# Projections in pairs on the same loaded weights, and a new static order

## The chip, the cores and the metric

The kernel runs on one core of a Trainium2 chip. The metric is the device time of one execution in microseconds, and the median of several runs is compared. The profile and the trace come from one further execution.

## The reference, cut to what matters

Four layers work on a sequence of 2048 tokens of width 512, with a layer norm before each and a residual sum after it: A, B, A, B, all with the same two sets of weights.

Layer A is attention by segments with a memory. The sequence is cut into 64 segments of 32 tokens, and 8 memory tokens stand ahead of each:

```python
for s in range(n_seg):
    h = jnp.concatenate([mem, xs], axis=1)
    q = jnp.einsum('btd,dhe->bhte', h, Wq)      # k and v likewise
    scores = jnp.einsum('bhqe,bhke->bhqk', q, k) * scale
    p = _softmax(jnp.where(mask[None, None], scores, -1000000000.0), axis=-1)
    o = jnp.einsum('bhqk,bhke->bhqe', p, v)
    o = jnp.einsum('bhte,hed->btd', o, Wo)
    mem = o[:, :M, :].copy()
    outs.append(o[:, M:, :])
```

There are 32 heads of 128. The memory of a segment comes out of the segment before it, so the segments form a chain. The memory rows may be seen by every token, and the 32 own tokens are masked causally.

Layer B is linear attention over the whole sequence: a projection to q, k and v (32 heads of 16), a feature map, one sum of k by v over all tokens, and a division.

## The kernel before, in words

**Tiles.** The 32 rows that a segment's step projects (8 memory tokens and the first 24 of its own) are the stationary operand of the matmul, `blk`, in four chunks of 128 features; the last 8 tokens of four segments are gathered into one "left" block of 32 rows, which is projected once for four segments (`left_block`). TensorE's array is used as four strips of 32 columns: a matmul has a `tile_position=(0, 32 * j)`, and four of them, one for each strip, run side by side on different columns of the weight matrix. Such four are called a group below. `project` (L1309) makes one product of 32 rows by 2048 columns, half of Wq, Wk or Wv: for each of the four chunks a group, each matmul with 512 moving columns, all into one PSUM bank. Every `pe.matmul` becomes two instructions of TensorE, a load of the stationary operand (LDWEIGHTS, row PEld in the profile) and the MATMUL itself. Each of the four strips loads the same 32 columns of `blk`.

**Steps of a segment in layer A.** `k0`, `k1`, `q0`, `q1`: the halves of k and q, each projected, evacuated from PSUM (L1150 on ScalarE or L1151 on VectorE) and turned by 32x32 blocks on VectorE (L1341, in `turned`). `v0`, `v1`: the halves of v, projected and evacuated. `mem0`, `mem1`: scores of both halves (L1417, L1423), exponentials, sums over the memory tokens with a matrix of ones as the stationary operand (`sums`, through `tiled`, L1261), and the weighted values. `out`: the projection with Wo (L1560). `next`: picks the memory rows for the next segment (L1584). `res`: residual rows, over a DMA from partition to partition on the GpSimd queue (L1595, L1166). `x`: the attention of the own tokens, off the memory's chain; its `sums` multiply a block matrix of ones, `bo_sb`, with two moving operands, 256 and 64 wide (L1498, L1494). Layer B's steps for each 128 tokens are `bi`, `bo`, `bm`, `bl`.

**What sets the order.** All is unrolled. Every operation has a key (layer, step, name, number), and two tables give each key a time: `PERIOD` for a repeating pattern of four segments, `OWN` for the steps outside it. `schedule` sorts all operations by these times, and that order is written to the five engines; the times have no other use. A letter behind a time says which engine evacuates, `a` for ScalarE and `v` for VectorE. Each engine runs its own list in order and waits on semaphores where an operand comes from another engine. Eight PSUM banks are given out in the order of the list: a tile takes the bank that came free first.

**At the start** the three matrices Wv, Wk and Wq (4 MB each) are fetched by DMAs that ScalarE issues, and Wo by SyncE after them.

Of the kernel before, what the change touches and what calls it, by code (L numbers as in the profile page):

```python
# [19 lines left out]
    0: (44811, 8548, {  # L20
# [3 lines left out]
        'k0': {  # L24
            0: '27075 27835 28266 28482 28937a 29591',
            1: '37951 38167 38382 38813 39593a 40223',
            2: '49129 49776 49991 50207 50833v 51555',
            3: '60060 60275 60491 60922 61377a 62008',
        },
        'k1': {  # L30
            0: '29460 29891 30106 30322 30777a 31461',
            1: '39244 39891 40106 40537 41172a 42855',
            2: '51284 52146 52362 52577 53033a 53663',
            3: '62430 62861 63077 63292 63748a 64508',
        },
        'q0': {
            0: '26213 26644 26860 28051 28506v 29229',
            1: '38598 39029 39460 39675 40382a 41013',
            2: '49560 50422 50853 51069 51524a 52155',
            3: '61137 61353 61784 62215 62670a 63301',  # L40
        },
        'q1': {
            0: '26429 27346 29244 29675 30131v 31099',
            1: '40322 40753 40968 41184 41653a 43217',
            2: '49345 50638 51715 51931 52386a 53137',
            3: '60706 61568 61999 62646 63152a 64146',
        },
        'v0': {
            0: '30537 31971 32314 32530 32985a',
            1: '41399 41743 41958 42174 42629a',  # L50
            2: '51500 52821 53036 53783 54238a',
            3: '63508 63723 63967 64498 65023a',
        },
        'v1': {
            0: '32849 33177 33392 33608 34063a',
            1: '42556 43050 43265 43896 44624a',
            2: '53567 54404 54675 55002 55754a',
            3: '64182 64852 65661 66044 66796a',
        },
        'ql': {  # L60
            0: '29419a 20723a',
            1: '38961a 39431a',
            2: '45732v 45838v',
            3: '56799a 59805a',
        },
# [5 lines left out]
        },  # L71
# [5 lines left out]
        },  # L77
        'out': {
# [4 lines left out]
        },  # L83
        'next': {
            0: '37244 37304 37674a',
            1: '48363 48423 48793a',
            2: '59078 59353 59723a',
            3: '70225 70341 70711a',
        },
        'res': {  # L90
            0: '37280 37736 38286 27562 28697 29026 30881 31099 31317 31535 31753 32211a 32372a 32683 35339 35889 36439 34789 33689 34239 36989 33139 41375',
            1: '48292 49298 48748',
            2: '60782 61788 61238',
            3: '72597 73054 73604',
        },
        'bi': {
            2: '41830 42777 43111 43458 43703 44222 41831 45054v 45612 45829 46275 46491 46947 48745 50087 69577 69794 78810 79242 80554v 82311 70401 91215 70771 81379 81604 81829 82537 83291 83921 84265 87192',
        },
# [5 lines left out]
        },  # L104
        'prep': {
            2: '14773 22863 25330 32839 45393 46045 46515a 51917v 54935a 49318a 49183a',
        },
        'left0': {
            2: '47795 48483 48698 48914 49453a 57204 47579 48147 53252 55489 57604a 58877',
        },  # L110
        'left1': {
            2: '58431 58862 59413 59844 60566a 64870 55273 56159 58647 59629 60084a 65510',
        },
        'leftv0': {
            2: '67011 68054 70010 70587 71042v 72121 75548',
        },
        'leftv1': {
            2: '59138 65445 66546 67226 68217a 76773 77947',
        },
        'lefts': {  # L120
            2: '77556 79138 79889 80348',
        },
    }),
    1: (47082, 762505, {
        'bo': {
            0: '1100 0 6030 6495 7750 10877 15245 17797 18014 18230 19216',
        },
        'k0': {
            0: '7730 8001 8217 8870 9325v 10048',
            1: '19150 19581 19797 20228 20683a 21314',  # L130
            2: '31406 31621 31892 32323 32779a 33409',
            3: '41870 42517 43594 44025 44481a 45111',
        },
        'k1': {
            0: '8432 11035 11466 11785 12241a 12871',
            1: '21736 21952 22167 22383 22838a 23469',
            2: '31190 32108 32970 33185 33641a 35120',
            3: '43810 45402 45617 45833 46288v 47539',
        },
        'q0': {  # L140
            0: '9085 9301 9516 9732 10187a 11484',
            1: '20012 20443 20659 20874 21330a 21960',
            2: '29897 30328 30544 30759 31215a 31845',
            3: '42301 42732 42948 43379 43834a 44465',
        },
        'q1': {
            0: '7299 7515 10819 11250 11706a 12336',
            1: '19366 21090 21305 21521 21997a 22628',
            2: '30113 30975 32539 33672 34127a 34758',
            3: '42086 43163 44241 44727 45590a 47177',  # L150
        },
        'v0': {
            0: '13105 13348 13664 13879 14335a',
            1: '22598 22842 23268 23484 23939a',
# [877 lines left out]
def _build_kernel(nc, A_x, A_mem0, A_Wq, A_Wk, A_Wv, A_Wo, A_seg_len, B_wqkv, B_wo, out):  # L1032
# [112 lines left out]
    add = P.add  # L1145
# [742 lines left out]
```

## Time and profile before

| what | value |
|---|---|
| median of 3 runs | 1713.43 us |
| lowest and highest | 1710.27 and 1716.99 us |
| the profiled execution | 1702.65 us |
| its span, first to last instruction | 1700.9 us |
| granted TensorE clock, mean | 0.992 |
| HBM read and written | 29.63 MB and 10.49 MB |

The span is what the profile's shares refer to. The profiled execution's own time is the span and what lies around it. It was an execution of its own, and not one of the three. PE and PEld are matmuls and weight loads of the same engine and overlap.

### The profile page before, as it was taken

Reading aid. Unit: us, or ns where it says so; the run is one execution under the profiler, and the core shown is the slowest. Engines: PE = TensorE matmul, PEld = TensorE weight load, DVE = VectorE, ACT = ScalarE, POOL = GpSimd, SP = SyncE. Lnnn points to the kernel's source line nnn. Section 1 sums busy time; section 2 is a strip of 40 time slices with the busy share of each in tenths; the row PEclk is TensorE's granted clock in tenths of the full one; section 3 lists DMA queues with packets and bytes.
Section 4 is the critical chain, followed back from the end, with each engine's and each line's share of the span. In section 5 each row is a group of like instructions: output and inputs, shape, how many; then the busy total and the mean of one; then the engine's idle time right before and its main releaser. Section 6 shows DMA issues by size and latency. Waiting matters only on the chain.

```text
span 1700.9 us, 115242 instructions
## 1 busy us (share of the span) xinstructions
PE 1555.4 (91%) x53257; PEld 1096.2 (64%) x53257; DVE 1170.0 (69%) x3811; ACT 1133.5 (67%) x3266; POOL 325.7 (19%) x660
## 2 busy tenths in 40 slices
PE   2999999998999999999799999999999999999896
PEld 0577667766666666676466666666667667666663
DVE  1677676766766676677567777767777777677776
ACT  0576676776767677676467677667677667776664
POOL 2022222122221112222101221121222121222120
PEclk9999999999999999999899999999999999999998
DMA  9200000000000000000000000000000000000013
GB/s 380 79 14 17 16 13 12 15 16 17 17 17 13 10 16 16 17 19 17 19 9 13 16 17 19 19 15 15 19 17 20 19 20 10 20 19 16 25 43 121
DMA packets 34930, 51.67 MB, mean 30 GB/s; under 512 B 13432, under 2 KB 28592, under 8 KB 32912
## 3 DMA queue, kind: packets, MB, share of 16 engines
q0 software_dynamic: 21744, 19.78, 4.1%
q1 hardware_dynamic: 11120, 11.94, 2.1%
q10 hardware_dynamic: 1584, 12.58, 1.8%
q8 instruction: 417, 6.83, 1.7%
q14 instruction: 65, 0.53, 0.1%
HBM read 29.63 MB, written 10.49 MB: 24 GB/s over the span
## 4 chain that ended last, share of the span: by engine, by line
PE 82%; DVE 6%; issue 6%; ACT 4%; DMA 2%; POOL 0%; DVEq 0%; ACTq 0%
PE pb L1318 30%; PE pb L1560 18%; PE pb L1261 14%; PE pb L1322 14%; ACT arena_sb L1150 2%; DMA Wq_sb<-in_A_Wq_dram 2%; PE pb L1417 2%; PE pb L1584 1%; DVE arena_sb L1151 1%; PE pb L1286 1%; DVE st_sb L1272 1%; DVE arena_sb L1444 1%; PE pb L1498 1%; DVE arena_sb L1341 1%; DVE Wq_sb L1829 0%
## 5 line engine op out<-in xcount | busy, mean ns | idle before, releaser
L1150 ACT ACTIVATE arena_sb<-pb 128x512 bf16<-128x512 f32 (+4 forms) x1303 | 603.5, 488 | 309.6 <-PE pb L1318 190.7
L1261 PE MATMUL pb<-arena_sb 128*32 128x128 bf16 (+2 forms) x14320 | 429.0, 224 | 28.6 <-issue 21.4
L1166 POOL DMA_DIRECT2D dx_sb<-y_sb x504 | 253.5, 509 | 1031.7 <-DVE y_sb L1595 674.3
L1318 PE MATMUL pb<-Wk_sb,arena_sb 128*32 128x512 bf16 x5120 | 437.3, 381 | 9.0 <-ACT arena_sb L1150 5.2
L1318 PE MATMUL pb<-Wq_sb,arena_sb 128*32 128x512 bf16 x5120 | 424.3, 380 | 22.3 <-DMA Wq_sb<-in_A_Wq_dram 20.1
L1322 PE MATMUL pb<-Wv_sb,arena_sb 128*32 128x512 bf16 x5120 | 415.2, 378 | 2.4 <-issue 1.7
L1560 PE MATMUL pb<-Wo_sb,arena_sb 128*32 128x256 bf16 x10368 | 372.0, 273 | 29.2 <-issue 26.0
L1261 PEld LDWEIGHTS pb<-arena_sb 128*32 128x32 bf16 x14320 | 283.8, 96 | 100.5 <-issue 34.2
L1341 DVE STREAM_TRANSPOSE arena_sb<-arena_sb 128x256 f32<-128x256 f32 x640 | 267.8, 433 | 108.4 <-ACT arena_sb L1150 99.9
L1560 PEld LDWEIGHTS pb<-Wo_sb,arena_sb 128*32 128x32 bf16 x10368 | 269.7, 96 | 75.3 <-issue 41.8
L1151 DVE CAST arena_sb<-pb 128x512 bf16<-128x512 f32 (+3 forms) x440 | 230.4, 527 | 103.7 <-PE pb L1318 64.2
L1318 PEld LDWEIGHTS pb<-Wq_sb,arena_sb 128*32 128x32 bf16 x5120 | 163.1, 97 | 109.8 <-DMA Wq_sb<-in_A_Wq_dram 20.3
L1318 PEld LDWEIGHTS pb<-Wk_sb,arena_sb 128*32 128x32 bf16 x5120 | 164.5, 97 | 103.3 <-issue 11.8
L1322 PEld LDWEIGHTS pb<-Wv_sb,arena_sb 128*32 128x32 bf16 x5120 | 143.9, 95 | 49.1 <-issue 4.3
L1150 ACT ACTIVATE outW_sb<-pb 128x128 fp32r<-128x128 f32 x290 | 66.1, 275 | 121.9 <-PE pb L1560 90.2
L1150 ACT ACTIVATE arena_sb<-arena_sb 32x256 bf16<-32x256 bf16 (+1 forms) x365 | 132.5, 363 | 13.4 <-DVE arena_sb L1505 8.2
L1466 DVE TENSOR_TENSOR arena_sb<-pb,arena_sb 128x128 bf16<-128x128 f32 x252 | 73.1, 291 | 71.5 <-PE pb L1261 48.0
L1444 DVE TENSOR_TENSOR arena_sb<-arena_sb 128x128 bf16<-128x128 bf16 x504 | 91.2, 215 | 28.9 <-ACT arena_sb L1434 24.9
L1595 DVE TENSOR_TENSOR y_sb<-pb,outW_sb 64x256 bf16<-64x256 f32 x158 | 65.9, 417 | 64.4 <-ACT outW_sb L1150 60.5
L1434 ACT ACTIVATE arena_sb<-pb 128x192 bf16<-128x192 f32 (+1 forms) x256 | 84.0, 329 | 25.1 <-PE pb L1417 21.5
L1151 DVE COPY arena_sb<-arena_sb 32x256 bf16<-32x256 bf16 (+1 forms) x403 | 82.0, 209 | 8.2
L1455 ACT ACTIVATE arena_sb<-arena_sb 128x128 f32<-128x128 f32 x252 | 78.1, 310 | 5.9
(99 smaller groups left out, 1564.1 us busy)
## 6 DMA issues: line engine op xcount, KB each, us to landing
Wv_sb<-in_A_Wv_dram ACTq DMA_DIRECT2D x1, 4096.0 KB, 13.7
Wk_sb<-in_A_Wk_dram ACTq DMA_DIRECT2D x1, 4096.0 KB, 23.1
Wq_sb<-in_A_Wq_dram ACTq DMA_DIRECT2D x1, 4096.0 KB, 33.5
Wo_sb<-in_A_Wo_dram SPq DMA_DIRECT2D x4, 1024.0 KB, 14.5
xs_scratch<-x_sb POOLq DMA_DIRECT2D x32, 128.0 KB, 2.1
pq_scratch<-arena_sb POOLq DMA_DIRECT2D x32, 128.0 KB, 2.0
dx_sb<-y_sb POOLq DMA_DIRECT2D x252, 12.0 KB, 1.9
dx_sb<-y_sb POOLq DMA_DIRECT2D x252, 4.0 KB, 1.9
```

Of the source, the lines that this page charges most:

```text
L1150: return e.activation(o() if callable(o) else o, i() if callable(i) else i, ACTF.Copy)
L1151: return e.tensor_copy(o() if callable(o) else o, i() if callable(i) else i)
L1166: add(eng, lambda e: e.dma_start(o, i), 0.55 if eng == "pool" else 0.4, reads=reads, writes=writes, dsem="%s%d" % (kind, k), lat=lat + (0. ...
L1261: r = pe.matmul(o[q], w[:, q], x, start=start, stop=stop, skip_group_check=True, tile_position=(0, 32 * j))
L1318: r = pe.matmul(tl.f32()[32 * j:32 * j + 32, 0:512].rearrange("p (i j f) -> p i j f", i=4, j=4), blk[:, c, :], w, start=(c == 0), stop=(c ...
L1322: r = pe.matmul(tl.f32()[32 * j:32 * j + 32, 0:512], blk[:, c, :], W[:, c, o:o + 512], start=(c == 0), stop=(c == 3), tile_position=(0, 32 ...
L1341: add("dve", lambda v: v.transpose(dst, src(img[:, k, :].bitcast(F32))), 0.445, reads=[("img", k)], writes=[dkey])
L1434: add("act", lambda a: a.activation(PQ[:, r2, b, 0:nq], tl.f32()[:, 0:nq], ACTF.Exp, scale=SCALE), c_act(nq), tiles=[tl], writes=[("PQ", r ...
L1444: add("dve", lambda v, a=a, p_=p_, w_=w_: v.tensor_tensor(wide(Pm[:, k, a, :]), p_.unsqueeze(2).to_broadcast([128, 4, 4, 8]), w_, ALU.mult ...
L1455: add("act", lambda a: a.activation(Rm[:, k, :], Rm[:, k, :], ACTF.Exp, scale=-1.0), c_act(128, 0, 1), reads=[("Rm", k)], writes=[("Rm", k)])
L1466: add("dve", lambda v: v.tensor_tensor(oTb[:, s % NO, 16 * b:16 * b + 16, 0:8], pv.f32()[:, 0:128].rearrange("p (n q) -> p n q", q=8), Rm[ ...
L1560: r = pe.matmul(tl.f32()[32 * j:32 * j + 32, 0:256], oT[:, 4 * hh + n, :], Wo_sb[:, 8 * n + hh, 256 * d:256 * d + 256], start=(hh == 0 and ...
```

## The change

**Pairs.** `project` takes several products of the same `blk`: for each chunk it issues the group of the first product as before, and then the group of the second, whose matmuls have no load of their own (`again`, with `ldweights=False`) and use the weights that the first group has put there. The pairs are the same halves of k and q (steps `kq0`, `kq1`, `left0`, `left1`) and the two halves of v (`v`, `leftv`). Both products keep a PSUM bank each, and their groups alternate. **Sums.** The second group of `sums` in `mem_attention`, and the second moving operand of the sums in `x_attention`, are issued without a load too, on the ones that the first has loaded. **Order.** Both tables are new throughout, the places of the evacuations on ScalarE or VectorE among them. At the start the order of the issues on ScalarE becomes Wv, Wq, Wk. What is computed stays the same.

```diff
--- before.py
+++ after.py
 PERIOD = {
-    0: (44811, 8548, {
+    0: (44811, 12408, {
...
-        'k0': {
-            0: '27075 27835 28266 28482 28937a 29591',
...
-        'q0': {
-            0: '26213 26644 26860 28051 28506v 29229',
...
+        'kq0': {
+            0: '15615 15683 15864 15888 16980v 17806 15947a 17085',
+            1: '26894 27017 27702 27828 29127a 29240 28510a 28790',
...
+        'v': {
+            0: '19217 19623 20563 20925 22429a 23133v',
...
@@ -1254,11 +1033,21 @@
     evac(memT0_sb[:, :, :], lambda tl=tl: tl.bf16()[:, 0:4 * M].rearrange("p (c m) -> p c m", m=M), 32, tiles=[tl],
          writes=["memT0"])
 
-    def tiled(pe, o, w, x, start, stop):
+    def again(pe, o, w, x, start, stop, tile_position, skip=False):
+
+        return pe.add_instruction(mybir.InstMatmult(
+            name=nc.get_next_instruction_name(), engine=mybir.EngineType.PE, ins=[pe.lower_ap(x), pe.lower_ap(w)],
+            outs=[pe.lower_ap(o)], start_tensor_calc=start, stop_tensor_calc=stop, tile_size=(128, 32),
+            tile_position=tile_position, bass_skip_group_check=skip, ldweights=False))
+
+    def tiled(pe, o, w, x, start, stop, loaded=False):
 
         for j in range(4):
             q = slice(32 * j, 32 * j + 32)
-            r = pe.matmul(o[q], w[:, q], x, start=start, stop=stop, skip_group_check=True, tile_position=(0, 32 * j))
+            if loaded:
+                r = again(pe, o[q], w[:, q], x, start, stop, (0, 32 * j), True)
+            else:
+                r = pe.matmul(o[q], w[:, q], x, start=start, stop=stop, skip_group_check=True, tile_position=(0, 32 * j))
         return r
 
     ln_no = [0]
@@ -1306,33 +1095,37 @@
             P.at(layer, s, name)
 
 
-        def project(W, key, blk, bkeys, b, urgent, across=False):
-            tl = P.tile()
+        def project(blk, bkeys, *parts):
+
+            tls = [P.tile() for _ in parts]
             for c in range(4):
 
                 def mm(pe, c=c):
-                    for j in range(4):
-                        if across:
-
-                            w = W[:, c, :].rearrange("p (j b i f) -> p b i j f", j=4, b=2, i=4)[:, b, :, :, 32 * j:32 * j + 32]
-                            r = pe.matmul(tl.f32()[32 * j:32 * j + 32, 0:512].rearrange("p (i j f) -> p i j f", i=4, j=4),
-                                          blk[:, c, :], w, start=(c == 0), stop=(c == 3), tile_position=(0, 32 * j))
-                            continue
-                        o = (8 * j + 4 * b) * DH
-                        r = pe.matmul(tl.f32()[32 * j:32 * j + 32, 0:512], blk[:, c, :], W[:, c, o:o + 512],
-                                      start=(c == 0), stop=(c == 3), tile_position=(0, 32 * j))
+                    for i, (tl, (W, key, b, across)) in enumerate(zip(tls, parts)):
+                        for j in range(4):
+                            o = tl.f32()[32 * j:32 * j + 32, 0:512]
+                            if across:
+
+                                w = W[:, c, :].rearrange("p (j b i f) -> p b i j f", j=4, b=2, i=4)[:, b, :, :, 32 * j:32 * j + 32]
+                                o = o.rearrange("p (i j f) -> p i j f", i=4, j=4)
+                            else:
+                                n = (8 * j + 4 * b) * DH
+                                w = W[:, c, n:n + 512]
+                            if i:
+                                r = again(pe, o, blk[:, c, :], w, c == 0, c == 3, (0, 32 * j))
+                            else:
+                                r = pe.matmul(o, blk[:, c, :], w, start=(c == 0), stop=(c == 3), tile_position=(0, 32 * j))
                     return r
-                add("pe", mm, 0.2155, reads=[key] + bkeys, tiles=[tl])
-            return tl
+                add("pe", mm, 0.2155 * len(parts), reads=sorted({p[1] for p in parts}) + bkeys, tiles=tls)
+            return tls
 
         def slot_img(urgent):
             k = img_no[urgent] % NI if urgent else NI + img_no[urgent] % NIL
             img_no[urgent] += 1
             return k
 
-        def turned(W, key, blk, bkeys, b, dst, dkey, urgent, src=None):
-
-            tl = project(W, key, blk, bkeys, b, urgent, True)
+        def turned(tl, dst, dkey, urgent, src=None):
+
             k = slot_img(urgent)
             nd = evac(img[:, k, :].rearrange("p (n f e) -> p n f e", f=32, e=2),
                       lambda: tl.f32()[:, :].rearrange("p (n e f) -> p n f e", f=32, e=2), 512, tiles=[tl],
@@ -1348,12 +1141,13 @@
             bk = [("hTl", r2)]
             for b in range(2):
                 at(step, "left%d" % b)
-                turned(Wq_sb, "Wq", blk, bk, b, pairs(qTl[:, r2, 4 * b:4 * b + 4]), ("qTl", r2, b), False)
-                turned(Wk_sb, "Wk", blk, bk, b, kTl[:, r2, b].rearrange("p g j c -> p (g j c)").bitcast(F32).rearrange("p (g n x) -> p n g x", g=4, n=8),
+                tq, tk = project(blk, bk, (Wq_sb, "Wq", b, True), (Wk_sb, "Wk", b, True))
+                turned(tq, pairs(qTl[:, r2, 4 * b:4 * b + 4]), ("qTl", r2, b), False)
+                turned(tk, kTl[:, r2, b].rearrange("p g j c -> p (g j c)").bitcast(F32).rearrange("p (g n x) -> p n g x", g=4, n=8),
                        ("kTl", r2, b), False, lambda v: v.rearrange("p (i j f) -> p j i f", i=4, j=2))
-            for b in range(2):
-                at(step, "leftv%d" % b)
-                tl = project(Wv_sb, "Wv", blk, bk, b, False)
+            at(step, "leftv")
+            tls = project(blk, bk, (Wv_sb, "Wv", 0, False), (Wv_sb, "Wv", 1, False))
+            for b, tl in enumerate(tls):
                 k = slot_img(False)
                 evac(img[:, k, :], lambda tl=tl: tl.f32()[:, :], 512, tiles=[tl], writes=[("img", k)])
                 add("dve", lambda v, k=k: v.transpose(
@@ -1447,7 +1241,7 @@
 
             def sums(pe):
                 for a in range(2):
-                    r = tiled(pe, tl.f32()[:, 256:384], one_sb, Pm[:, k, a, :], a == 0, a == 1)
+                    r = tiled(pe, tl.f32()[:, 256:384], one_sb, Pm[:, k, a, :], a == 0, a == 1, a == 1)
                 return r
             add("pe", sums, 0.112, reads=[("Pm", k, 0), ("Pm", k, 1), "one"], tiles=[tl])
             add("act", lambda a: a.activation(Rm[:, k, :], tl.f32()[:, 256:384], ACTF.Ln), c_act(128), tiles=[tl],
@@ -1491,9 +1285,8 @@
                         q = slice(32 * j, 32 * j + 32)
                         o = tl.f32()[q, 0:256].rearrange("p (b i q) -> p b i q", b=2, i=4)
                         if left:
-                            r = pe.matmul(o[:, :, :, 24:32], bo_sb[:, q],
-                                          PLL[:, g2, :, g, :].rearrange("p b (i q) -> p b i q", i=4), start=False, stop=True,
-                                          tile_position=(0, 32 * j))
+                            r = again(pe, o[:, :, :, 24:32], bo_sb[:, q],
+                                      PLL[:, g2, :, g, :].rearrange("p b (i q) -> p b i q", i=4), False, True, (0, 32 * j))
                         else:
                             pe.matmul(o, bo_sb[:, q], px, start=True, stop=False, tile_position=(0, 32 * j))
                 return r
@@ -1668,14 +1461,12 @@
             if g == 0 and G + 1 < NT:
                 tokens(G + 1, s)
             for b in range(2):
-                at(s, "k%d" % b)
-                turned(Wk_sb, "Wk", blk, bk, b, pairs(kT[:, 4 * b:4 * b + 4]), ("kT", b), True)
-            for b in range(2):
-                at(s, "q%d" % b)
-                turned(Wq_sb, "Wq", blk, bk, b, pairs(qT[:, 4 * b:4 * b + 4])[:, :, 0:32], ("qT", b), True)
-            for b in range(2):
-                at(s, "v%d" % b)
-                tl = project(Wv_sb, "Wv", blk, bk, b, True)
+                at(s, "kq%d" % b)
+                tk, tq = project(blk, bk, (Wk_sb, "Wk", b, True), (Wq_sb, "Wq", b, True))
+                turned(tk, pairs(kT[:, 4 * b:4 * b + 4]), ("kT", b), True)
+                turned(tq, pairs(qT[:, 4 * b:4 * b + 4])[:, :, 0:32], ("qT", b), True)
+            at(s, "v")
+            for b, tl in enumerate(project(blk, bk, (Wv_sb, "Wv", 0, False), (Wv_sb, "Wv", 1, False))):
                 evac(vimg[:, r2, 512 * b:512 * b + 512], lambda tl=tl: tl.f32()[:, :], 512, tiles=[tl],
                      writes=[("v", r2, b)])
             for b in range(2):
```

More of the change, by code (lines that the diff above doesn't have):

```diff
@@ L48 @@
[L48 to L58, printed above, removed]
[5 rows of a table added]
+        },
[5 rows of a table added]
+        },
+        'v': {
+            0: '19217 19623 20563 20925 22429a 23133v',
+            1: '29021 29057 29620 30152 31739a 33681a',
+            2: '39986 39990 40130 40204 42111a 42388v',
+            3: '50779 51826 51878 52330 52930a 54191v',
@@ L88 @@
-            3: '70225 70341 70711a',
+            0: '26273 26339 26881a',
+            1: '36204 36238 36468v',
+            2: '46730 47134 47214v',
+            3: '57443 58931 59528v',
         },
         'res': {
[L91 to L94, printed above, removed]
+            0: '26413 29085 28578 16827 17928 18059 19472 19628 20197 20285 20348 21183a 21065a 22119 22471 27054 25376 26149 25457 26865 26429 27486 29298',
@@ L95 @@
+            1: '35892 36378 40637',
+            2: '48040 55875 49042',
+            3: '59913 64111 66644',
         },
         'bi': {
-            2: '41830 42777 43111 43458 43703 44222 41831 45054v 45612 45829 46275 46491 46947 48745 50087 69577 69794 78810 79242 80554v 82311 70401 91215 70771 81379 81604 81829 82537 83291 83921 84265 87192',
+            2: '29579 29639 30252 30485 31074 31754 36111 32464v 32525 32660 33085 33116 34682 36633 37296 66776 67142 67250 70746 72173v 72241 72289 72853 76618 67948 70897 71368 72184 72696 73303 73304 77201',
@@ L113 @@
         },
[L114 to L118, printed above, removed]
+        'leftv': {
+            2: '53105 54166 57081 57233 60621a 62076 62878 61336a 64749 65324',
         },
         'lefts': {
-            2: '77556 79138 79889 80348',
+            2: '59226 61319 63743 67375',
         },
     }),
-    1: (47082, 762505, {
+    1: (47442, 832763, {
         'bo': {
-            0: '1100 0 6030 6495 7750 10877 15245 17797 18014 18230 19216',
+            0: '1645 545 7432 9078 10688 13525 18153 18369 18585 18978 19960',
@@ L140 @@
[L140 to L151, printed above, removed]
@@ L192 @@
-            3: '53664 53724 54094v',
+            0: '18802 18885 19288v',
+            1: '29716 29799 30169a',
+            2: '42011 42071 42441a',
+            3: '54323 54383 54753v',
         },
         'res': {
-            0: '18510 18966 19516 9947 10165 10383 10601 12001 12451 12669 12887 13345a 13506a 13831 14287 14837 17587 17037 15937 18137 16487 15387 22990',
-            1: '30654 31110 31660',
-            2: '40965 41422 47632',
-            3: '54881 55337 55887',
+            0: '19507 21792 21242 13185 13403 14292 14510 14728 14946 15164 15382 16002a 15840a 16386 18492 17392 19592 20142 16842 19042 20692 17942 24928',
```

92 lines of the change are left out of this document (26 added, 66 removed), and 998 rows, old and new, of tables (OWN, PERIOD).

## The prediction

> **What bounds the kernel now.** I read the page first: shares of the engines, queues, chain.
>
> ```profile
> span 1700.9 us, 115242 instructions
> PE 1555.4 (91%) x53257; PEld 1096.2 (64%) x53257; DVE 1170.0 (69%) x3811; ACT 1133.5 (67%) x3266; POOL 325.7 (19%) x660
> ...
> q8 instruction: 417, 6.83, 1.7%
> ...
> PE 82%; DVE 6%; issue 6%; ACT 4%; DMA 2%; POOL 0%; DVEq 0%; ACTq 0%
> ```
>
> TensorE is the bound, and each of its 53,257 matmuls has a weight load of its own. Two things in these lines are easily passed over. "Issue", time in which an engine waits for nothing that the profile shows, is 6% of the chain, 102 us. And queue q8 moved 417 packets of instructions: 53,257 + 53,257 = 106,514 TensorE instructions over 417 are 255.4, so a packet (16 KB) brings 256 of them, 128 matmuls with their loads.
>
> Next I asked for the timeline of PE around one such stall (start, duration, count of matmuls; in brackets the idle time before).
>
> ```profile
> 342.27 0.60 PE L1560 MATMUL pb<-Wo_sb,arena_sb 128*32 128x256 bf16 x13
> 344.52 1.38 PE L1560 MATMUL pb<-Wo_sb,arena_sb 128*32 128x256 bf16 x43 [1.65 <-issue]
> 345.64 0.88 PE L1261 MATMUL pb<-arena_sb 128*32 128x128 bf16 x45
> 346.31 0.21 PE L1584 MATMUL pb<-selm_sb,outW_sb 128*32 128x16 f32 x2
> 346.35 0.23 PE L1261 MATMUL pb<-arena_sb 128*32 128x128 bf16 x3
> 346.41 0.30 PE L1584 MATMUL pb<-selm_sb,outW_sb 128*32 128x16 f32 x14
> 346.54 0.29 PE L1498 MATMUL pb<-arena_sb,bo_sb 128*32 128x256 bf16 x4
> 346.64 0.21 PE L1494 MATMUL pb<-arena_sb,bo_sb 128*32 128x64 bf16 x4
> 346.67 0.39 PE L1261 MATMUL pb<-arena_sb 128*32 128x128 bf16 x13
> 348.00 0.46 PE L1261 MATMUL pb<-arena_sb 128*32 128x128 bf16 x19 [0.94 <-issue]
> ```
>
> From the end of one stall to the end of the next, 43+45+2+3+14+4+4+13 = 128 matmuls start, exactly one packet of instructions, in 348.00 - 344.52 = 3.48 us, though they stream for only 3.48 - 0.94 = 2.54 us. I read this as a floor: a page of 256 instructions can't be replaced faster than about every 3.4 to 3.5 us, and a page with less matmul time in it than that leaves TensorE idle for the rest.
>
> The Trainium skill, Runtime: NRT & Kernel Launch, section Instruction fetch mechanics, also has blocks of 256 instructions, but calls crossing one mostly hidden; the 0.94 us above disagree, and the trace decides here.
>
> Then the loads beside the matmuls, in a stretch of projections, and rows from which a group of four (one for each 32 columns of the array) gets its pace.
>
> ```profile
> 399.96 0.12 PEld L1318 LDWEIGHTS pb<-Wq_sb,arena_sb 128*32 128x32 bf16 x4
> 400.17 0.12 PEld L1318 LDWEIGHTS pb<-Wk_sb,arena_sb 128*32 128x32 bf16 x4
> 400.17 0.40 PE L1318 MATMUL pb<-Wq_sb,arena_sb 128*32 128x512 bf16 x4
> 400.39 0.40 PE L1318 MATMUL pb<-Wk_sb,arena_sb 128*32 128x512 bf16 x4
> 400.60 0.83 PE L1318 MATMUL pb<-Wq_sb,arena_sb 128*32 128x512 bf16 x12
> ...
> 603.78 0.41 PE L1286 MATMUL pb<-id_sb,arena_sb 128*32 128x128 bf16 x16
> 604.00 0.84 PE L1560 MATMUL pb<-Wo_sb,arena_sb 128*32 128x256 bf16 x24
> 604.66 0.30 PE L1261 MATMUL pb<-arena_sb,one_sb 128*32 128x128 bf16 x8
> ```
>
> The 512-wide groups follow each other by 0.215 us, and the four loads of the next one have run 0.2 us earlier. So in a dense stretch a load costs nothing, and taking it away gains nothing there. 128-wide groups go at (604.00 - 603.78) / 4 = 0.055 us, 256-wide ones at 0.66 / 6 = 0.110.
>
> **The change part by part.** First, how many loads go. The groups by line and shape:
>
> ```profile
> L1318 PE MATMUL pb<-Wk_sb,arena_sb 128*32 128x512 bf16 x5120 | 437.3, 381 | 9.0 <-ACT arena_sb L1150 5.2 <-issue 3.4 <-DVE arena_sb L1151 0.2
> L1318 PE MATMUL pb<-Wq_sb,arena_sb 128*32 128x512 bf16 x5120 | 424.3, 380 | 22.3 <-DMA Wq_sb<-in_A_Wq_dram 20.1 <-issue 1.6 <-DVE arena_sb L1151 0.3
> L1322 PE MATMUL pb<-Wv_sb,arena_sb 128*32 128x512 bf16 x5120 | 415.2, 378 | 2.4 <-issue 1.7 <-ACT outW_sb L1150 0.5 <-ACT arena_sb L1150 0.2
> L1560 PE MATMUL pb<-Wo_sb,arena_sb 128*32 128x256 bf16 x10368 | 372.0, 273 | 29.2 <-issue 26.0 <-DVE arena_sb L1744 0.5 <-DVE arena_sb L1466 0.2
> L1261 PE MATMUL pb<-arena_sb 128*32 128x128 bf16 x8960 | 307.5, 219 | 19.5 <-issue 15.6 <-ACT arena_sb L1150 1.8 <-DVE arena_sb L1151 0.5
> L1261 PE MATMUL pb<-arena_sb,one_sb 128*32 128x128 bf16 x2016 | 77.2, 219 | 3.7 <-DVE arena_sb L1444 3.2 <-issue 0.3
> L1494 PE MATMUL pb<-arena_sb,bo_sb 128*32 128x64 bf16 x512 | 29.8, 193 | 0.4 <-issue 0.2
> ```
>
> Half of the 15,360 projections reuse weights: 7,680 loads. Half of the 2,016 sums over ones: 1,008. All 512 second products of the block sums at L1494. Together 9,200, or 2,300 groups of four, and 97,314 TensorE instructions stay: 380 pages for 416.
>
> **The streaming time** does not change: 3,840 projection groups at 0.2157, 2,592 at L1560 at 0.109, 2,240 and 504 128-wide ones at 0.0557 are 1,264 us, the smaller rows priced likewise 204, together 1,468 us.
>
> **The fetches** do. I laid TensorE's work in the order of the tables in the diff (sorted by their times, which I used for nothing else) into pages of 256 instructions, gave each group its pace from above, and counted every page at its streaming time or 3.4 us, whichever is more, averaged over 16 places of the first boundary, which the trace does not show. Before: 1,619.9 us; 230 of 416 pages are under 3.4 us, short by 151.6 in all. That such a sum holds is seen in the two steady stretches:
>
> ```profile
> 60.00:795.00 735.00, 693.29 (x24244) 503.12 (x24240) 512.14 (x1720) 511.67 (x1498) 143.65 (x282) 1.00 0.06 15
> 870.00:1645.00 775.00, 734.75 (x25435) 516.26 (x25428) 553.91 (x1818) 538.97 (x1568) 153.06 (x298) 1.00 0.06 17
> ```
>
> Counted from the order of the trace, the same sum gives 734.9 us for the first 735.0 and 768.4 for the second 775.0 (bare streaming: 663.9 and 699.2). So 3.4 is the value that I take, below the 3.48 of the one page, since what is queued ahead covers a little.
>
> After: 1,554.2 us; 153 of 380 pages are short, by 85.9. That is 65.7 us less. Loads taken out in the old order would give 1,574.1 (45.8 less), the new order with all loads kept 1,592.8 (27.1 less). With a floor of 3.3 the whole is 57.9, with 3.5 it is 73.5: the bounds.
>
> **The pairs** move the second product ahead to the first. Two PSUM tiles then end together, 1.72 us after the start, where one ended every 0.86. What is late next: the evacuations. Per segment k and q keep their cover: at least 1.4 us of TensorE work (before 1.2) between the last projection and the first score matmul. The v pair loses some: before, at least 0.97 us of work lay between its end and the first reader for the first half; now the median of 126 is 0.94, a quarter is under 0.79, the least 0.22.
>
> ```profile
> L1150 ACT ACTIVATE arena_sb<-pb 128x512 bf16<-128x512 f32 x800 | 464.5, 595 | 226.1 <-PE pb L1318 190.7 <-PE pb L1261 13.6 <-DVE arena_sb L1151 5.6
> L1151 DVE CAST arena_sb<-pb 128x512 bf16<-128x512 f32 x204 | 139.5, 685 | 69.1 <-PE pb L1318 64.2 <-PE pb L1261 2.2 <-PE pb L1322 0.8
> ```
>
> An evacuation takes 0.595 us on ACT, 0.685 on DVE, and begins 0.380 - 0.215 = 0.165 after the pace of the group, so it needs about 0.8 us. Some 50 of 126 steps are short, by about 0.25: 12 us. A page already at the floor hides this, 153 of 380, so I take 8 us. Behind the waiting reader the queue of PE stands. The tables also give DVE 152 more evacuations of projections: 1,170 + 152 x 0.685 = 1,274 us less what moves to ACT, still under 80% of the span. Bounds of all of this: nothing, and 30 us, if out and next, whose covers shrink by 0.1 us, give back as much again in both layers.
>
> **Nothing is priced** for the start: the first projection waits 20.1 us for the last of three weight arrays, and a pair of q and k needs that one too, whichever is issued last; if it were v's turn meanwhile, the order has none there. The layer change and the end keep their instructions. POOL's row moves are reordered, with TensorE not waiting for them in the rows above.
>
> **The sum.** The profiled execution took 1702.65 us, 10.8 under the median of 1713.43. 1702.65 - 65.7 + 8 = 1645, and 10.8 more for a median: 1656 us.
>
> **The rivals.** (1) Slower: a matmul on weights already loaded costs extra. The trace has none without a load, so the price is open: at least nothing, at most what a group lasts beyond its pace, 0.380 - 0.215 = 0.165 us, were it not overlapped. 2,300 times that is 380 us, 2036 us in all. It decides from 58 / 2300 = 0.025 us on. For it: nothing measured. Against: in the rows at 400.17 and 400.39 the loads are long done when the matmuls start, so the pace there is set by the moving width alone.
>
> (2) Waits take the place of the fetches. The static order was paced by stalls everywhere; without them the chain from a segment's memory tokens to the next segment's shows up, DVE above all. Against: the rows above lay only some us on DVE and ACT ahead of PE. Two thirds given back: 1690 us.
>
> (3) The stalls are not of the fetch but of something that the same work causes; then 36 fewer pages change nothing: 1713 us. Against it stand the exact 128. By the Trainium skill's page Runtime: NRT & Kernel Launch, named above, fetches are hidden, and this case would follow.
>
> (4) Loads do stand in the way of matmuls. Four take 0.12 us in the rows at 399.96 and 400.17; 2,300 times that is 276 us, 1713 - 276 = 1437 us. The pace of 0.215 with loads speaks against it. The Trainium skill, TensorE: Matmul & The Clock Gate, in Part 3, The mechanism, says that a load overlaps running matmuls only where row groups differ, and here all use all 128 rows; by that it would follow, but the trace does not agree.
>
> **How the numbers follow.** Forecast 0.74, with its own range from 1713 - 73.5 = 1640 to 1713 - 57.9 + 30 = 1685; rival 1 0.07, rival 2 0.11, rival 3 0.05, rival 4 0.03. The range 1635 to 1695 takes in the bounds and most of rival 2. About 0.5% is what a measurement of this kernel can tell from no change. Faster: 0.74 + 0.03 + 0.10 of rival 2 = 0.87; same 0.05 + 0.01 = 0.06; slower 0.07.
>
> **What would show it.** Loads at 44,057 beside 53,257 matmuls; q8 at 381 packets or so; issue waits of PE well down, those before L1560 and L1261 first; the 512-wide groups of a pair at 0.215 us still. Wrong: second groups that start later than that (1), longer DVE and ACT waits ahead of L1261 and L1560 (2), or stalls as before with fewer packets (3).

## The result and the profile after

The changed kernel takes 1658.03 us as a median of 4 runs (1652.04 to 1660.09), the kernel before 1714.36 us beside it (1710.27 to 1716.99): a ratio of 0.9668, 95% interval 0.9635 to 0.9700. 1656 us were forecast. In two later comparisons the ratio was 0.9651 (0.9617 to 0.9685) and 0.9659 (0.9634 to 0.9683); 0.966 stands for the changed kernel below. Its profiled execution took 1659.31 us.

The page of the changed kernel: span, engines, instruction queue, chain.

```profile
span 1657.6 us, 105934 instructions
PE 1551.8 (94%) x53257; PEld 884.8 (53%) x44057; DVE 1276.4 (77%) x4017; ACT 1067.1 (64%) x3060; POOL 325.4 (20%) x660
...
q8 instruction: 381, 6.24, 1.6%
...
PE 79%; ACT 8%; DVE 7%; DMA 3%; issue 2%; POOL 1%; ACTq 0%; DVEq 0%
```

The same 53,257 matmuls now have 44,057 loads, 9,200 fewer, and 381 packets of instructions came instead of 417. "Issue" went from 6% of the chain to 2%, and ACT from 4% to 8%.

What PE waited for between 60 and 1600 us, first the kernel before (columns: total us, times, longest), where L1261 is the helper `tiled` and L1560 the projection with Wo:

```profile
PE pb L1261 <- issue: 25.0, 36, 1.4
PE pb L1560 <- issue: 20.6, 32, 2.1
PE pb L1286 <- DVE arena_sb L1278: 5.5, 2, 2.7
PE pb L1584 <- issue: 5.5, 10, 1.1
PE pb L1318 <- ACT arena_sb L1150: 5.2, 16, 0.4
PE pb L1318 <- issue: 5.0, 8, 1.3
PE pb L1286 <- issue: 4.2, 7, 0.8
```

and the changed kernel, where `tiled` is L1050, Wo L1353, and L1238 the product that makes the sums' operand:

```profile
PE pb L1050 <- DVE arena_sb L1238: 8.1, 17, 2.0
PE pb L1050 <- ACT arena_sb L929: 5.9, 18, 0.5
PE pb L1075 <- DVE arena_sb L1067: 5.7, 2, 2.9
PE pb L1353 <- issue: 4.2, 10, 0.8
PE pb L1050 <- DVE arena_sb L930: 3.7, 15, 0.5
PE pb L1050 <- issue: 3.1, 9, 0.5
PE pb L1117 <- ACT arena_sb L929: 2.9, 13, 0.3
```

The five issue rows of before held 60.3 us; the two largest now hold 7.3. All rows of this view added up, issue fell from 64.7 to 10.7 us, while the waits on VectorE and ScalarE grew from 21.9 to 35.4.

The timeline of PE and PEld shows the pairs (L1117 loads its weights, L1038 is the second group without a load):

```profile
400.27 0.39 PE L1117 MATMUL pb<-Wq_sb,arena_sb 128*32 128x512 bf16 x4
400.49 0.39 PE L1038 MATMUL pb<-Wk_sb,arena_sb 128*32 128x512 bf16 x4
400.71 0.39 PE L1117 MATMUL pb<-Wq_sb,arena_sb 128*32 128x512 bf16 x4
400.92 0.39 PE L1038 MATMUL pb<-Wk_sb,arena_sb 128*32 128x512 bf16 x4
...
400.17 0.11 PEld L1117 LDWEIGHTS pb<-Wq_sb,arena_sb 128*32 128x32 bf16 x4
400.49 0.11 PEld L1117 LDWEIGHTS pb<-Wq_sb,arena_sb 128*32 128x32 bf16 x4 [0.22 <-issue]
```

The groups start 0.21 to 0.22 us apart, with or without a load of their own, as in the kernel before. Nothing was gained inside a pair and nothing lost.

### The profile page after: what moved, and what is told of

Its sections match the earlier page's. It is cut to its first block, busy times and chain, and to the rows that moved or that the text cites. A ratio compares the mean times of both kernels' runs of the same rounds, so it can differ in the third digit from the quotient of the medians.

```text
span 1657.6 us, 105934 instructions
## 1 busy us (share of the span) xinstructions
PE 1551.8 (94%) x53257; PEld 884.8 (53%) x44057; DVE 1276.4 (77%) x4017; ACT 1067.1 (64%) x3060; POOL 325.4 (20%) x660
## 4 chain that ended last, share of the span: by engine, by line
PE 79%; ACT 8%; DVE 7%; DMA 3%; issue 2%; POOL 1%; ACTq 0%; DVEq 0%
PE pb L1117 22%; PE pb L1038 22%; PE pb L1353 16%; PE pb L1050 13%; ACT arena_sb L929 5%; DMA Wk_sb<-in_A_Wk_dram 2%; DVE arena_sb L930 2%; PE pb L1377 2%; PE pb L1211 1%; DMA dx_sb<-y_sb 1%; DVE arena_sb L1134 1%; POOL dx_sb L945 1%; PE pb L1075 1%; PE pb L1291 1%; ACT outW_sb L929 1%
## 5 line engine op out<-in xcount | busy, mean ns | idle before, releaser
L929 ACT ACTIVATE arena_sb<-pb 128x512 bf16<-128x512 f32 (+6 forms) x1068 | 505.2, 500 | 284.7 <-PE pb L1038 213.7
L1050 PE MATMUL pb<-arena_sb 128*32 128x128 bf16 (+2 forms) x14320 | 404.0, 224 | 23.3 <-ACT arena_sb L929 7.3
L1117 PE MATMUL pb<-Wk_sb,arena_sb 128*32 128x512 bf16 x4096 | 413.5, 380 | 5.6 <-ACT arena_sb L929 2.9
L1038 PE MATMUL pb<-Wq_sb,arena_sb 128*32 128x512 bf16 x4096 | 413.3, 379 | 0.0
L930 DVE CAST arena_sb<-pb 128x512 bf16<-128x512 f32 (+3 forms) x647 | 335.0, 522 | 95.7 <-PE pb L1038 49.9
L1050 PEld LDWEIGHTS pb<-arena_sb 128*32 128x32 bf16 x14320 | 273.2, 96 | 200.6 <-issue 73.8
L1353 PE MATMUL pb<-Wo_sb,arena_sb 128*32 128x256 bf16 x10368 | 345.1, 273 | 6.7 <-issue 4.5
L1353 PEld LDWEIGHTS pb<-Wo_sb,arena_sb 128*32 128x32 bf16 x10368 | 264.2, 96 | 61.2 <-issue 17.8
L1117 PE MATMUL pb<-Wv_sb,arena_sb 128*32 128x512 bf16 x2560 | 257.7, 378 | 0.1
L1038 PE MATMUL pb<-Wv_sb,arena_sb 128*32 128x512 bf16 x2560 | 257.6, 379 | 0.0
L1117 PEld LDWEIGHTS pb<-Wk_sb,arena_sb 128*32 128x32 bf16 x4096 | 124.7, 97 | 213.8 <-issue 169.3
L929 ACT ACTIVATE arena_sb<-arena_sb 32x256 bf16<-32x256 bf16 (+1 forms) x409 | 153.2, 378 | 22.8 <-DVE arena_sb L1298 17.2
L1117 PE MATMUL pb<-Wq_sb,arena_sb 128*32 128x512 bf16 x1024 | 107.4, 387 | 23.0 <-DMA Wk_sb<-in_A_Wk_dram 22.4
L1117 PEld LDWEIGHTS pb<-Wv_sb,arena_sb 128*32 128x32 bf16 x2560 | 76.6, 96 | 74.1 <-issue 55.7
L1228 ACT ACTIVATE arena_sb<-pb 128x192 bf16<-128x192 f32 (+1 forms) x256 | 83.8, 328 | 44.4 <-PE pb L1211 25.7
L929 ACT ACTIVATE outW_sb<-pb 128x128 fp32r<-128x128 f32 x274 | 61.9, 274 | 78.1 <-PE pb L1353 75.5
L1238 DVE TENSOR_TENSOR arena_sb<-arena_sb 128x128 bf16<-128x128 bf16 x504 | 92.7, 213 | 23.5 <-ACT arena_sb L1228 19.6
L1038 PE MATMUL pb<-Wk_sb,arena_sb 128*32 128x512 bf16 x1024 | 106.9, 386 | 0.0
```

Source lines behind the costliest of these rows:

```text
L929: return e.activation(o() if callable(o) else o, i() if callable(i) else i, ACTF.Copy)
L930: return e.tensor_copy(o() if callable(o) else o, i() if callable(i) else i)
L1038: return pe.add_instruction(mybir.InstMatmult(name=nc.get_next_instruction_name(), engine=mybir.EngineType.PE, ins=[pe.lower_ap(x), pe.low ...
L1050: r = pe.matmul(o[q], w[:, q], x, start=start, stop=stop, skip_group_check=True, tile_position=(0, 32 * j))
L1117: r = pe.matmul(o, blk[:, c, :], w, start=(c == 0), stop=(c == 3), tile_position=(0, 32 * j))
L1228: add("act", lambda a: a.activation(PQ[:, r2, b, 0:nq], tl.f32()[:, 0:nq], ACTF.Exp, scale=SCALE), c_act(nq), tiles=[tl], writes=[("PQ", r ...
```

## The experiments

The theory: TensorE's instructions come in pages of 256, a page is not replaced faster than every 3.4 us or so, and a page with less matmul time than that leaves the engine idle. Removed loads pay as removed instructions. Rivals: the loads stood in the array's way; the new order alone made the gain; new waits set the pace.

**All loads put back, new order kept.**

```diff
     def again(pe, o, w, x, start, stop, tile_position, skip=False):
 
+        return pe.matmul(o, w, x, start=start, stop=stop, skip_group_check=skip, tile_position=tile_position)
```

> The changed kernel in its new order, with every one of the 9,200 loads put back (each matmul loads its own weights again; nothing else differs). Theory of the fetches: 36 more pages of 256 TensorE instructions, and by the sum over pages with a floor of 3.4 us 38.6 us more than the changed kernel (33.7 to 44.4 with 3.3 and 3.5), less what waits already cover, so 1685 to 1702 us beside 1658; the pace inside a pair of 512-wide groups stays at 0.215 us. Theory that loads stand in the way of matmuls: 0.12 us for each of 2,300 groups of four, 276 us more, and a slower pace in the pairs. Theory that the order alone made the gain: 1658 us.

Measured: 1701.92 us beside 1706.13 for the kernel before, a ratio of 0.9977 (0.9960 to 0.9993). The order alone is worth 0.2%. How much the loads are worth in it is less sure, since the changed kernel was not run beside it and the kernel before was 8 us faster here than in the other comparisons: 54 us by the ratios (0.9977 against 0.966), 44 to 49 by the bare medians (1701.92 against 1653 to 1658), where 39 were expected (34 to 44). Loads in the array's way would have been 276 us. The waits of PE between 60 and 1600 us in this kernel (`tiled` is L1051, Wo L1354, L1239 the product for the sums):

```profile
PE pb L1051 <- issue: 14.8, 33, 1.0
PE pb L1354 <- issue: 11.4, 25, 0.9
PE pb L1051 <- DVE arena_sb L1239: 8.8, 18, 1.8
PE pb L1051 <- ACT arena_sb L929: 6.0, 18, 0.5
```

Here is what became of the order's own gain. With the same 417 packets as before, all issue rows together fell from 64.7 to 37.3 us, 27.4 less, where the sum over pages had 27.1. But the waits on the other engines are 35.6 us instead of 21.9, the same new rows as in the changed kernel. They took back half of it, and the measured difference of the kernels is 4 us; where the remaining 10 us went, these rows don't show.

**The projections' loads alone put back.**

```diff
-                            if i:
-                                r = again(pe, o, blk[:, c, :], w, c == 0, c == 3, (0, 32 * j))
-                            else:
+                            if True:
                                 r = pe.matmul(o, blk[:, c, :], w, start=(c == 0), stop=(c == 3), tile_position=(0, 32 * j))
```

> As the changed kernel, with the 7,680 loads of the projections alone put back; the sums keep their saved loads. Theory of the fetches: 30 pages more, 21.5 us more by the sum over pages (18 to 26), about 1678 us, and the same time as the kernel with 7,680 fillers in these places. Theory that the load itself costs time in the array: slower than the kernel with fillers.

Measured: 1680.62 us, ratio 0.9864 (0.9828 to 0.9900), for 7,680 loads. By the ratios that is 35 us over the changed kernel, by the bare medians 23 to 27, so 3 to 4.5 ns for a load; 21.5 were expected (18 to 26). As above, the changed kernel was not run beside it, and whether the size was missed stays open.

**The sums' loads alone put back.**

```diff
-                    r = tiled(pe, tl.f32()[:, 256:384], one_sb, Pm[:, k, a, :], a == 0, a == 1, a == 1)
+                    r = tiled(pe, tl.f32()[:, 256:384], one_sb, Pm[:, k, a, :], a == 0, a == 1)
...
-                            r = again(pe, o[:, :, :, 24:32], bo_sb[:, q],
...
+                            r = pe.matmul(o[:, :, :, 24:32], bo_sb[:, q],
...
```

> The changed kernel with the 1,520 loads of the sums alone put back. Theory of the fetches: 6 pages more, but in the densest stretches, where short groups follow each other, so 15 us more than the changed kernel (14 to 16 by the sum over pages), that is 10 ns a load beside 3 to 4 ns for a projection's. Theory that every load costs alike, whatever surrounds it: 1,520 times 4.4 ns, 7 us more.

Measured: 1671.69 us, ratio 0.9748 (0.9723 to 0.9774) beside 0.9659 of the changed kernel in the same comparison: 15 us for 1,520 loads, 10 ns each, as the sum over pages has it. A load among short groups is worth two to three times one among projections. That every load costs alike falls.

**The old order, with the loads left out.**

```diff
+                    lone = P.last is not None and P.last[2] not in ("next", "res", "setup") and (
+                        name in ("q0", "q1", "v1", "leftv1") or (name in ("left0", "left1") and key == "Wk"))
...
+                            if lone:
+                                r = again(pe, y, blk[:, c, :], w, c == 0, c == 3, (0, 32 * j))
+                            else:
+                                r = pe.matmul(y, blk[:, c, :], w, start=(c == 0), stop=(c == 3), tile_position=(0, 32 * j))
```

> The kernel before in its old order, with the loads of q0, q1, v1, the left block's k and second v half, and of the second sums simply left out: 9,008 loads fewer. These matmuls use whatever weights are there, so their values are not the reference's; only the time counts. Theory of the fetches: 45 us less than the kernel before, about 1669 us (40 to 51 less). Theory that the new order made the gain: no change from 1714 us. Theory that a matmul without its own load costs extra: slower than 1714 us.

Measured: 1657.82 us beside 1706.13, ratio 0.9722 (0.9696 to 0.9748): 48 us less, where 45 were expected. The removed loads make nearly the whole gain, without any pair and without the new order, which adds 0.6% to them. Its timeline also tells what a page counts. Between the ends of two stalls (L1582 is Wo, L1274 `tiled`, L1338 projections with loads, L1262 all matmuls without):

```profile
386.73 0.51 PE L1582 MATMUL pb<-Wo_sb,arena_sb 128*32 128x256 bf16 x12 [0.71 <-issue]
387.06 0.86 PE L1274 MATMUL pb<-arena_sb 128*32 128x128 bf16 x48
387.73 0.32 PE L1606 MATMUL pb<-selm_sb,outW_sb 128*32 128x16 f32 x16
387.88 0.29 PE L1520 MATMUL pb<-arena_sb,bo_sb 128*32 128x256 bf16 x4
387.98 0.21 PE L1262 MATMUL pb<-arena_sb,bo_sb 128*32 128x64 bf16 x4
388.01 0.63 PE L1274 MATMUL pb<-arena_sb 128*32 128x128 bf16 x32
388.46 0.83 PE L1338 MATMUL pb<-Wk_sb,arena_sb 128*32 128x512 bf16 x12
389.10 0.40 PE L1262 MATMUL pb<-Wq_sb,arena_sb 128*32 128x512 bf16 x4
390.48 0.40 PE L1338 MATMUL pb<-Wk_sb,arena_sb 128*32 128x512 bf16 x4 [0.98 <-issue]
```

12+48+16+4+4+32+12+4 = 132 matmuls, no longer 128; 8 of them (L1262) have no load, so there are 124 loads, and 132 + 124 = 256 instructions again, in 3.75 us.

The traces also hold the start and the duration of every instruction packet, and they tell what the stalls wait for. In the kernel before, TensorE stands idle for 0.5 us or more at 62 places between 60 and 1600 us. At 55 of them the next matmul starts 1.2 to 1.6 us after a packet has landed; of random moments one in ten would. For the two stalls in the prediction, which end at 344.52 and 348.00, the packets landed at 343.22 and 346.64. All 55 also stand at the same place in a page: the loads, matmuls and semaphore waits ahead of them, counted from the kernel's start, leave 192 or 193 when they are divided by 256. In the changed kernel 11 such places are left, and 3 of them fit. Two packets never start less than 3.2 us apart between 60 and 1600 us, in any of the kernels here.

**Fillers.** To part the instruction from the load, fillers were put in that do nothing: waits for a value long reached, first ahead of each matmul without a load, then ahead of each pair.

```diff
                             if i:
+                                for _ in range(2):
+                                    pe.wait_ge(P.sems["pe"], 1)
                                 r = again(pe, o, blk[:, c, :], w, c == 0, c == 3, (0, 32 * j))
...
+                    for _ in range(9):
+                        pe.wait_ge(P.sems["pe"], 1)
                     for i, (tl, (W, key, b, across)) in enumerate(zip(tls, parts)):
```

Of these waits one or two ride along with each instruction; one and four extra instructions stay.

> The changed kernel with no load put back, but one more TensorE instruction ahead of each of the 7,680 projection matmuls without a load: a wait for a semaphore value that was reached at the start. It touches neither the array nor SBUF. Theory of the fetches: an instruction is an instruction, so the time of the kernel with the projections' loads put back, 1678 us (21.5 more, 18 to 26), and 30 more packets in the instruction queue. Theory that the loads themselves were the cost: 1658 us as without fillers.

> The changed kernel with the fillers in another place: four more TensorE instructions (waits on a value long reached) ahead of each pair of groups, so that the four strips of a group still start together. Theory of the fetches: the time of the kernel with the projections' loads put back, 0.986 of the kernel before, that is 22 to 34 us over the changed kernel. Theory that a removed load saved time in the array: as the changed kernel. If a filler costs about 30 ns of the sequencer's own, as the 230 us for 7,680 fillers between the matmuls suggest, and nothing covers it: 230 us over the changed kernel again, and then this says nothing on the fetches.

Measured: 1887.59 us (ratio 1.1075, 1.1043 to 1.1107) and 1872.85 us (1.0931, 1.0896 to 1.0967, beside 0.9651 of the changed kernel). The first was expected at 1678 us, the time with the projections' loads put back, and missed this by 210 us, though the packets came as expected: 411 and, in the second kernel, 412, for 381 without fillers. The second is 0.128 of 1715, 220 us, over the changed kernel; its trace has 7,950 waits more, so a filler cost 28 ns on average. The timeline of PE with the fillers ahead of the pairs:

```profile
400.25 0.40 PE L1119 MATMUL pb<-Wk_sb,arena_sb 128*32 128x512 bf16 x4
400.46 0.40 PE L1038 MATMUL pb<-Wq_sb,arena_sb 128*32 128x512 bf16 x4
400.69 0.40 PE L1119 MATMUL pb<-Wk_sb,arena_sb 128*32 128x512 bf16 x4
...
401.44 0.23 PE L1050 MATMUL pb<-arena_sb 128*32 128x128 bf16 x4
401.91 0.40 PE L1119 MATMUL pb<-Wv_sb,arena_sb 128*32 128x512 bf16 x4 [0.25 <-PE pb L1050]
```

Where a pair follows a pair, the fillers cost little: 0.44 us a pair here, beside 0.43 in the changed kernel. Behind short groups the engine sits idle. In the trace two fillers in a row start 0.106 us apart, so four of them take 0.42 us of TensorE's instruction stream; the 0.43 us of a pair's matmuls cover that, short groups don't. So the times of both runs say nothing on the fetches, as the second expectation had allowed for. The places of the stalls do: of the stalls of 0.5 us or more that end 1.2 to 1.6 us after a packet has landed, 32 of 33 in the first kernel and 28 of 28 in the second again leave 192 to 194 instructions over 256, with the fillers counted. A page counts loads, matmuls and waits alike.

**Memory values from the v of the segment before**, so that nothing waits for the evacuation of the v pair.

```diff
+            r0 = 1 - r2 if s else r2
...
-                    r = tiled(pe, pv.f32()[:, o], vimg[:, r2, 128 * hh:128 * hh + 128], Pm[:, k, 0, o], False, i == 3)
+                    r = tiled(pe, pv.f32()[:, o], vimg[:, r0, 128 * hh:128 * hh + 128], Pm[:, k, 0, o], False, i == 3)
...
-            add("pe", pvm, 0.176, reads=[("Pm", k, 0), ("Pm", k, 1), ("v", r2, b), ("vl", g2, b)], tiles=[pv])
+            add("pe", pvm, 0.176, reads=[("Pm", k, 0), ("Pm", k, 1), ("v", r0, b), ("vl", g2, b)], tiles=[pv])
```

> The changed kernel, but the weighted values of the memory tokens are computed from the v of the segment before, which is there long since, so nothing waits for the evacuation of the v pair; values differ from the reference from the second segment on. Theory that the thin cover of the v pair is what the new order gives back: 8 to 12 us less than the changed kernel. Theory that the waits lie elsewhere (the sums' operand on VectorE, the memory rows): no change, within 4 us.

Measured: 1653.37 us beside 1653.40, ratio 0.9650 (0.9620 to 0.9680): no change. The waits of PE between 870 and 1600 us, first in the changed kernel, then here:

```profile
PE pb L1050 <- DVE arena_sb L1238: 7.2, 14, 1.9
PE pb L1050 <- ACT arena_sb L929: 4.6, 14, 0.3
```

```profile
PE pb L1050 <- DVE arena_sb L1238: 14.5, 14, 2.7
PE pb L1050 <- issue: 3.5, 7, 1.1
```

The wait for the evacuation (L929) is gone, and its time has moved to the next wait, for the operand of the sums. The same 14 places show in the timeline of the changed kernel, once in four segments of the second layer A:

```profile
998.60 0.28 PE L1211 MATMUL pb<-arena_sb 128*32 128x40 bf16 x16
...
998.73 0.60 ACT L929 ACTIVATE arena_sb<-pb 128x512 bf16<-128x512 f32 x1 [0.44 <-PE pb L1038]
...
999.38 0.45 PE L1050 MATMUL pb<-arena_sb 128*32 128x128 bf16 x28 [0.34 <-ACT arena_sb L929]
999.38 0.34 ACT L1228 ACTIVATE arena_sb<-pb 128x192 bf16<-128x192 f32 x1
...
999.75 0.23 DVE L1238 TENSOR_TENSOR arena_sb<-arena_sb 128x128 bf16<-128x128 bf16 x1
...
1000.24 0.24 PE L1050 MATMUL pb<-arena_sb,one_sb 128*32 128x128 bf16 x4 [0.40 <-DVE arena_sb L1238]
```

Behind the evacuation of v on ScalarE, with one short operation between, stands the exponential of the scores (L1228), then the product on VectorE (L1238), then TensorE's sums. The scores (L1211) end at 998.88, and the exponential begins at 999.38: the evacuation delays all three, whether or not the first reader of v waits for it. This is read from the trace; no run puts the exponential ahead of the evacuation.

**The v pair evacuated on ScalarE alone.**

```diff
+    t, eng = planned(key, engs)
+    return t, "act" if key[2] == "v" and "act" in engs else eng
...
+def planned(key, engs):
```

> The changed kernel with all evacuations of the v pair on ScalarE; about half of them were on VectorE, which stands at 77% of the span and ScalarE at 64%. Theory that VectorE's queue gives rise to the new waits: 5 to 15 us less than the changed kernel. Theory that the two evacuations of a pair must run side by side: as long as before or up to 10 us longer, since the second half of v now comes 0.6 us later.

Measured: 1678.84 us, ratio 0.9804 (0.9773 to 0.9834), 26 us more than the changed kernel, beyond both expectations. That VectorE's load makes the waits falls: with less on VectorE (1204 us busy for 1276) the time grew. The waits of PE between 60 and 1600 us (the places L1055, L934 and L1243 are `tiled`, ScalarE's evacuation and the sums' product):

```profile
PE pb L1055 <- DVE arena_sb L1243: 15.6, 46, 0.8
PE pb L1055 <- ACT arena_sb L934: 11.3, 33, 1.0
```

Both have about doubled against the 8.1 and 5.9 of the changed kernel. A queue of ScalarE that has no room, with the exponentials in it, would do this. But the two halves of v are now also evacuated one after the other, and the run does not part the two causes.

**Still more loads left out.** The pairs' first groups of kq1, v, left1 and leftv go without loads too.

```diff
-                            if i:
+                            if i or P.now[2] in ("kq1", "v", "left1", "leftv") and P.last[2] not in ("next", "res", "setup", "prep", "bi"):
                                 r = again(pe, o, blk[:, c, :], w, c == 0, c == 3, (0, 32 * j))
```

> The changed kernel with 4,720 further loads left out: the first groups of kq1, v, left1 and leftv use whatever weights are there too, so the values are not the reference's. Theory of the fetches: 18 pages fewer, 12 us less by the sum over pages. Theory that waits on VectorE and ScalarE now set the pace: no gain, within 4 us.

Measured: 1644.66 us, ratio 0.9595 (0.9569 to 0.9620), 11 us less than the 0.9659 beside it, where 12 were expected. The fetches still set a part of the pace in the changed kernel. The values are not the reference's, so this is a measure and no better kernel. A last run of the changed kernel itself served as the measure of these two comparisons:

> The changed kernel as it is, as the measure for the two below: 0.965 to 0.967 of the kernel before.

and one more, in the same way, for the runs with fillers ahead of the pairs and with the v pair:

> The changed kernel as it is, on the chip of the three below, as their measure: 0.967 of the kernel before, as in the first comparison.

They gave the 0.9659 and 0.9651 above.

## Why the prediction was right, point by point

**The fetches as the second bound: right.** Packets 417 to 381, loads 44,057, issue waits almost gone, and nearly all long stalls of the kernel before stand at one place of a page and end 1.2 to 1.6 us after a packet. The sum over pages forecast four differences within 3 us: loads left out in the old order 45 against 48, the sums' loads 15 against 15, further loads 12 against 11, and the order's share of the issue waits 27 against 27. For the projections' loads in the new order it gave 21.5 against 23 to 35, for all loads there 39 against 44 to 54; how far it was too low stays open.

**Streaming time and the price of a matmul without a load: right.** The pace stayed at 0.215 us, and rival 1 with its price of 0.025 us or more is out. So is rival 4: nothing is won by a load less in a dense stretch.

**The split of the gain: half right.** The loads' 45.8 us came. The order's 27.1 us came too, as less issue, but did not stay: the run with all loads is 4 us faster than the kernel before, not 27, nor 19 with the 8 us for waits taken off. The loads in the new order made up for it, with 44 to 54 us where the sum had 39. That the two nearly cancel is luck.

**What is given back: wrong in place, and right in size by luck.** By medians the changed kernel gained 56, 62 and 59 us in the three comparisons, 4 to 9 less than the 65.7 of the sum over pages; the step "so I take 8 us" had 8. The spans of the profiled executions would give 22: 1700.9 - 1619.9 = 81 us before, 1657.6 - 1554.2 = 103 after. But that rests on single executions, and those of the kernel before lie between 1700 and 1720 us; two further profiled executions of the changed kernel span 1650.1 and 1653.5 and would give 15 and 18. The place was not the one that the step priced, the thin cover of the v pair: without the reader's wait the time stays. The prediction had the queue of TensorE behind the waiting reader, but not what stands behind the evacuation on its own engine, the exponential that the chain needs. Rival 2 named VectorE for such waits; the run with the v pair on ScalarE alone speaks against it.

**The offset is no forecast of its own.** "10.8 more for a median" leads from the one profiled execution back to the median: 1713.43 - 65.7 + 8 is the same 1656. The forecast is thus a difference of medians, and as such it held.

**Rival 3**, that pages make no difference, is refuted by the three runs in which nothing but loads changed, and by the packets in the trace.

## What to carry to other kernels

Where TensorE runs many short matmuls, count its instructions in pages of 256 and compare each page's matmul time with the 3.4 us that served for a new page here: a load hidden in the array can still cost 2 to 10 ns as an instruction, most among short groups. Spread the short groups between long ones, and let a second matmul use loaded weights where the operand is shared. When two products end together, look at what stands behind their evacuations in the queues of ScalarE and VectorE, not at their readers alone. Compare medians: one profiled execution lay 11 us from them here, as much as the waits that were to be told from its span.

## What the hardware showed that was not expected

A wait for a value long reached is not a free instruction on TensorE: two in a row started 0.106 us apart. Behind long matmuls this hid: with four fillers between, a pair behind a pair started 0.229 us after the group before it, as a median, for 0.216 without. Behind other groups it did not, 0.155 us for 0.055. And a page has more than one time. From the end of one stall to the end of the next it took 3.48 us in the page shown of the kernel before and 3.75 in that of the old order without loads, while the packets themselves never started less than 3.2 us apart.
